# Random-feature attention and a two-layer network on one core: another order of the work, eight buffers for a tile's sums, and matmuls of 256 columns in the second layer

## The chip, the cores and the metric

The kernel runs on one core of a Trainium2 chip. A core has TensorE (matmuls, written PE in the profile, its weight loads PEld), VectorE (DVE), ScalarE (ACT), GpSimd (POOL), and SyncE (SP), whose queue issues every DMA of this kernel. The metric is the time of one execution on the device in microseconds (us). Three runs of the kernel before took 992.41, 993.01 and 994.23 us; the median, 993.01 us, is the number to compare with. A change of under 0.2% can hardly be told from none.

## The reference

For each of 8 batches and 8 heads, with 576 rows of 64 values, the reference computes attention through 128 random features, then a normalization and a two-layer network over all 4608 rows of 512 values, and adds the network's input to its output:

```python
def phi(x):
    proj = np.einsum('bhsd,md->bhsm', x, omega)
    h = proj - np.sum(x * x, axis=-1, keepdims=True) / 2.0
    h = h - np.max(h, axis=-1, keepdims=True)
    return np.exp(h) / np.sqrt(m)
q_p, k_p = phi(q * scale), phi(k * scale)
kv = np.einsum('bhsm,bhsd->bhmd', k_p, v);  z = np.sum(k_p, axis=2)
num = np.einsum('bhsm,bhmd->bhsd', q_p, kv)
x = num / (np.einsum('bhsm,bhm->bhs', q_p, z)[..., None] + 1e-06)     # then (8, 576, 512)
xn = (x - mean) / np.sqrt(var + 1e-06) * g_ln
out = x + np.maximum(xn @ w_ch1, 0.0) @ w_ch2                        # 512 -> 2048 -> 512
```

All of it is in float32 with random inputs.

## The kernel before

**Tiles.** The 4608 rows are cut into nine tiles of 512 rows (`t`), each of four chunks of 128 rows (`i`). The hidden layer has 2048 columns, sixteen blocks of 128 (`f`). The two layers are done in fp32r matmuls, each operand split into a rounded part and the remainder, and a product is three passes: rounded by rounded, and the two mixed ones.

**First layer.** Tiles 0 and 1 use it plainly (`mm1`, 12 matmuls of 512 columns per `f`). Tiles 2 to 8 use a seven-product scheme on 2 by 2 blocks (`seven`, `product` at L1033): seven operands made from the transposed rows (`ORDER`: B11, T2, T1, T3, B21, B22, N4) meet seven weight operands, three taken from the weights as they are and four from sums of weights. Each product is 6 matmuls of 256 columns. A block `(g, h)` gives two hidden blocks and takes 42 matmuls; a tile has eight such blocks.

**Second layer.** `mm2` (L1166) multiplies one hidden block with one block of the second weights: for each of four chunks three passes, 12 matmuls of 512 columns, all through the helper `rounded` (L989, recorded as L991). It adds up in four PSUM banks over all sixteen `f`; `result` (L1189) then adds `x`, frees the bank and stores.

**The weight sums.** `gen_sides` (L420) makes the four sums of first-layer weights for each of four groups `g` and two halves `k`, starting when the rows it reads are loaded. Its DVE work is at L432 (16 times), L439 (32) and, in `lesser`, L456 (16). The sums go to DRAM; `gen_ring` (L477) loads them again, sixteen loads of 512 KB per tile.

**Lent weights.** Some blocks of the second weights give up their place in SBUF after tile 1. `SHARED` lists them: the places of blocks 4, 5 and 6 hold operands of the seven products, that of 7 holds partial sums `u`, those of 2 and 3 hold staging buffers `y0` to `y3`. Each such block `a` then takes turns with block `a + 8` in the place of `a + 8`: both are stored once (`gen_leave`, L400) and loaded once per tile (`gen_return`, L406), issued from SP.

**From rows to operands.** The DVE normalizes a chunk (`gen_xnT`, L862). For tiles 2 to 8 `gen_turned` (L908) transposes it on PE (L917), ACT copies it into a `y` buffer (L922). Chunks come in the order 0, 2, 1, 3. With a pair (0, 2) or (1, 3) both there, four subtractions (L938) fill two more `y` buffers, and `parted` (L958) writes each of the seven operands as rounded part and remainder (L962 through the helper at L231 or L233, and L964) as soon as the operand's buffer is free from the tile before. Since one pair fills all four `y` buffers, chunks 1 and 3 wait until every operand has taken its part of the first pair.

**Attention of the next tiles** runs beside the network: `gen_q2` loads queries (L678), splits them (L683 on ACT, L685 on DVE) and multiplies with omega; `features` takes the maximum over partitions on GpSimd (`partition_all_reduce`, L714), subtracts it on DVE (L717) and takes the exponential on ACT (L720). `gen_k` does the keys (L617, L548, L554, L586), `gen_x` the quotient (L784 to L817).

**The order.** The program's instruction order on each engine is fixed before it runs, by a list scheduler (`Plan`). Every step is a generator that yields what it needs: a wait for a key, buffers, or time on an engine with a cost in us. `Plan.run` takes the earliest possible start on each engine and, among those ready, the lowest `rank`; where two engines can do a step, `starts` (L154) chooses. The costs shape only this order. On the chip each engine takes its instructions strictly in it, waiting on semaphores for what really is not ready. Ranks: the network's rectifications and sums -2000, the transposes -1000 and up, attention of tile `t` about 32t - 28, the weight sums 24 to 27, the network's matmuls 10000, so that these fill what is left of PE.

Of the kernel before, what the change touches and what calls it, by code (L numbers as in the profile page):

```python
# [68 lines left out]
class Plan:  # L69
# [10 lines left out]
    HOP = 0.2  # L80
    SAME = {ACT: 0.16, DVE: 0.13, POOL: 0.1}
    SLACK = 0.4
    FILL, IDLE = 10000, 20000
    HOLDER = 100
    BIAS = {PE: 0.0, ACT: 0.2, DVE: 0.5, POOL: -0.2, SP: 0.0}
# [67 lines left out]

    def starts(self, part, queue):  # L154

        times = ((max(part.ready(e), self.free_at[e]), e, cost) for e, cost in part.want[1].items())
        return min(times, key=lambda t: t[0] + t[2] + queue[t[1]])

    def run(self):
# [31 lines left out]
def favor_ffn(ctx, tc, kT, kTr, vF, vR, qT, qD, omT, gT, w1, w2, out):  # L191
# [27 lines left out]

    def dve(n, k=1, c=0.065):  # L220
        return "run", {DVE: k * (c + 0.00105 * n)}

    def us(eng, t):
        return "run", {eng: t}
# [195 lines left out]
    def gen_sides(g, k):  # L420


        for row in (k, k + 2):
            yield wait("w", 1, NK * g + row)
        if g + k:
            yield wait("read", *((g, 0) if k else (g - 1, 1)))
        tags = yield "get", n_big, 4
        low, high, a, b = (tile_of(x, [P, 2, HC], F32R) for x in tags)
        for x, row in ((low, k), (high, k + 2)):
            yield dve(DM)  # L430
            w = wparts[1, NK * g + row]
            nc.vector.tensor_tensor(out=f32(x), in0=f32(w[:, :, 0]), in1=f32(w[:, :, 1]), op=ALU.add)  # L432
        low, high, a, b = f32(low), f32(high), f32(a), f32(b)
        for out, left, right, op in (
            (a[:, 0], low[:, 1], high[:, 1], ALU.add), (a[:, 1], low[:, 0], low[:, 1], ALU.subtract),
            (b[:, 0], a[:, 0], low[:, 0], ALU.subtract), (b[:, 1], high[:, 0], b[:, 0], ALU.subtract),
        ):
            yield dve(HC)
            nc.vector.tensor_tensor(out=out, in0=left, in1=right, op=op)  # L439
        if (g, 0) not in sides:  # L440
            sides[g, 0] = dp.tile([P, 4, 2, 2, HC], F32, tag=f"side{g}", name=f"side{g}", bufs=1)
        done(("read", g, k))
        for n in range(2):
            plan.add(plan.cur.rank, halved(g, k, n, tags[n], tags[2 + n], (a, b)[n]))

    def halved(g, k, n, t_h, t_s, s):
        hi = tile_of(t_h, [P, 2, HC], F32R)
        eng = yield "run", {ACT: 0.56, DVE: 0.34}
        copy(eng, hi, s)
        yield dma(P * DM)  # L450
        nc.sync.dma_start(sides[g, 0][:, 2 * n : 2 * n + 2, 0, k], f32(hi))
        plan.add(plan.cur.rank, lesser(g, k, n, t_s, s, hi, t_h))

    def lesser(g, k, n, t_s, s, hi, t_h):
        yield dve(DM)
        nc.vector.tensor_tensor(out=s.bitcast(F32R), in0=s, in1=f32(hi), op=ALU.subtract)  # L456
        free(t_h)
        yield dma(P * DM)
        nc.sync.dma_start(sides[g, 0][:, 2 * n : 2 * n + 2, 1, k], s)
        free(t_s)  # L460
        done(("side", g, n, k))
# [210 lines left out]
    def gen_q2(blk, j, s):  # L672
        rank = plan.cur.rank
        q_turn = yield "get", turn["q"]
        t_q = yield "get", n_big
        qraw = tile_of(t_q, [P, 2 * QB])
        yield dma(P * 2 * QB)
        nc.sync.dma_start(qraw, qD[blk, j, s])  # L678
        yield wait("om2")
        t_s = yield "get", n_big  # L680
        qs = tile_of(t_s, [P, 2 * QB], F32R)
        yield act(2 * QB)
        nc.scalar.copy(out=qs, in_=qraw)  # L683
        yield us(DVE, 0.85)
        nc.vector.tensor_tensor(out=qs[D:P], in0=qraw[D:P], in1=f32(qs[D:P]), op=ALU.subtract)  # L685
        free(t_q, q_turn)
        t_b = yield "get", at_now()

        plan.cur.after = max(plan.cur.after, plan.cur.end + LATE)
        yield us(PE, 0.46)  # L690
        pq = bank(t_b)
        rounded(pq, om_hi, qs, start=True, stop=False)
        rounded(pq, om_lo, qs, start=False, stop=True)
        free(t_s)
        yield from features(blk, j, s, t_b, pq)
# [8 lines left out]
    def features(blk, j, s, t_b, pq):  # L704
        t_c = yield "get", n_big
        qc = tile_of(t_c, [P, 2 * QB])
        eng = yield "run", {ACT: 0.48, DVE: 0.62} if blk >= T // QB else {ACT: 0.58}
        copy(eng, qc, pq)
        free(t_b)
        mx_turn = yield "get", turn["mx"]  # L710
        t_m = yield "get", n_big
        mx = tile_of(t_m, [P, 2 * QB])
        yield us(POOL, 1.9)
        nc.gpsimd.partition_all_reduce(mx, qc, P, bass_isa.ReduceOp.max)  # L714
        done(("mx", blk, j, s))
        yield us(DVE, 0.95 if blk >= T // QB else 0.6)
        nc.vector.tensor_tensor(out=qc, in0=qc, in1=mx, op=ALU.subtract)  # L717
        free(t_m, mx_turn)
        yield act(2 * QB)
        nc.scalar.activation(out=qc, in_=qc, func=AF.Exp)  # L720
        phis[blk, j, s] = t_c, qc.rearrange("p (a b) -> p a b", b=QB)
        done(("phi", blk, j, s))
# [127 lines left out]
    def gen_xnT():  # L850
        for n in range(NC):
            t, i = divmod(n, TC)
            i = i if t < SEVEN else i // 2 + i % 2 * 2
            c = t * TC + i
            plan.cur.rank = URGENT + t
            yield wait("x", c)
            xn_turn = yield "get", turn["xn"]
            t_n = yield "get", n_big
            _, x, mu, rs = xs[c]
            xn = tile_of(t_n, [P, DM])  # L860
            yield us(DVE, 0.34)
            nc.vector.tensor_scalar(out=xn, in0=x, scalar1=mu, scalar2=rs, op0=ALU.subtract, op1=ALU.mult)  # L862
            done(("xn", c))
            if t >= SEVEN:
                plan.add(plan.cur.rank, gen_turned(t, i, xn, t_n, xn_turn))
                continue
            if i == 0:
                t_t = yield "get", n_xnT
                xnTs[t] = t_t, tile_of(t_t, [P, 2, NK, T], F32R)
            plan.add(plan.cur.rank, gen_xnT1(t, i, xn, t_n, xn_turn))  # L870
# [22 lines left out]
            op_at[f"o{i}"] = whole[:, i]  # L893
            free(f"o{i}")

    n_y, y_at = ("y0", "y1", "y2", "y3"), {}

    def gen_staged():
        yield wait("mm1", SEVEN - 1, 0)
# [7 lines left out]

    def gen_turned(t, i, xn, t_n, xn_turn):  # L908

        if i % 2:  # L910
            for name in ORDER:
                yield wait("x2", t, name, 0)
        t_b = yield "get", at_now()
        yield us(PE, 0.46)
        pt = bank(t_b).rearrange("p (a b) -> p a b", b=P)
        for k in range(NK):
# [7 lines left out]
        turned[t, i] = t_f, xf  # L924
        done(("turned", t, i))
        if i < 2:
            plan.add(plan.cur.rank, parted(t, "B11", i, xf[:, 0]))
            plan.add(plan.cur.rank, parted(t, "B21", i, xf[:, 1]))
            return
        i -= 2  # L930
        yield wait("turned", t, i)
# [5 lines left out]
        def less(out, left, right):  # L937
            nc.vector.tensor_tensor(out=out, in0=left, in1=right, op=ALU.subtract)  # L938

        rank = plan.cur.rank  # L940
        yield dve(HC)
        less(a[:, 0], xf[:, 0], xe[:, 0])
        yield dve(HC)
        less(a[:, 1], xf[:, 1], a[:, 0])
        plan.add(rank, parted(t, "T2", i, a[:, 1]))
        plan.add(rank, parted(t, "T1", i, a[:, 0]))
        yield dve(HC)
        less(c[:, 0], xf[:, 1], xf[:, 0])
        plan.add(rank, parted(t, "T3", i, c[:, 0]))
        plan.add(rank, parted(t, "B22", i, xf[:, 1]))  # L950
        yield dve(HC)
        less(c[:, 1], xe[:, 1], a[:, 1])
        plan.add(rank, parted(t, "N4", i, c[:, 1]))
        for name in ORDER:
# [3 lines left out]
    def parted(t, name, i, x):  # L958
        yield wait("op", t, name)
        o = ops[t, name][1]  # L960
        eng = yield "run", {ACT: 0.3, DVE: 0.28}
        copy(eng, o[:, 0, :, i * P : (i + 1) * P], x)  # L962
        yield dve(HC)
        nc.vector.tensor_tensor(  # L964
            out=o[:, 1, :, i * P : (i + 1) * P], in0=x, in1=f32(o[:, 0, :, i * P : (i + 1) * P]), op=ALU.subtract
        )
        done(("x2", t, name, i))

    def gen_xnT1(t, i, xn, t_n, xn_turn):
# [8 lines left out]
        pt = pt.rearrange("p k (a b) -> p k a b", b=BW)  # L978
        yield us(ACT, 0.5)
        nc.scalar.copy(out=xnT[:, 0], in_=pt)  # L980
        yield dve(DM)
        nc.vector.tensor_tensor(out=xnT[:, 1], in0=pt, in1=f32(xnT[:, 0]), op=ALU.subtract)  # L982
        free(t_b)
        done(("xnT", t, i))
# [141 lines left out]
    def halves(hl, cols, x):  # L1126
        yield act(x.shape[1], 1, 0.05)
        nc.scalar.activation(out=hl[:, 0, cols], in_=x, func=AF.Relu)  # L1128
        yield dve(x.shape[1])
        nc.vector.scalar_tensor_tensor(  # L1130
            out=hl[:, 1, cols], in0=x, scalar=0.0, in1=f32(hl[:, 0, cols]), op0=ALU.max, op1=ALU.subtract
        )
# [33 lines left out]
    def mm2(t, f):  # L1166
# [7 lines left out]
        for i in range(TC):  # L1174
            if f == 0:
                t_b = yield "get", (b_acc[i],)
                accs[i] = bank(t_b)
            yield us(PE, 3 * 0.225)
            cs = slice(i * P, (i + 1) * P)
            rounded(accs[i], hl[:, 0, cs], w[:, 0], start=(f == 0), stop=False)  # L1180
            rounded(accs[i], hl[:, 0, cs], w[:, 1], start=False, stop=False)
            rounded(accs[i], hl[:, 1, cs], w[:, 0], start=False, stop=(f == NF - 1))
            if f == NF - 1:
                plan.add(MOST_URGENT, result(t, i, accs[i]))
        free(t_h)
        if lent and t >= SEVEN - 1:
            free(*n_w[2, f + HOSTS if t >= SEVEN and f in SHARED else f])
# [85 lines left out]
WHOLE = 4  # L1273
LATE = 1.0
SEVEN, HC = 2, DM // 2
SHARED, HOSTS = (4, 5, 6, 7, 2, 3), 8
LENT = (*SHARED, *(f + HOSTS for f in SHARED))
LEAVE, RSIDE = 24, 24
WARM, COLD = 0.0, 5.0
# [47 lines left out]
```

## Time and profile before

| | |
|---|---|
| Median of three runs | 993.01 us |
| The profiled execution | 995.0 us |
| Its span, first to last instruction | 993.1 us |
| PE busy | 975.7 us (98%), 7816 matmuls |
| DVE busy | 680.4 us (69%) |
| ACT busy | 417.2 us (42%) |
| POOL busy | 139.7 us (14%) |
| DMA | 180.81 MB, 182 GB/s on average |
| Mean granted TensorE clock | 0.998 |

A row of a group reads: line, engine, operation, tiles written <- read, partitions x elements, count, then busy us, mean ns of one, and idle time before it. In a timeline row the first number is the start in us from the start of the span, the second the length to the end of the last instruction of the row. Matmuls overlap: one of 256 columns is shown as about 275 ns long although the next begins earlier, so the rate is read from starts, not from lengths. A row of the windows view gives, for one stretch, the busy us of the engines and in brackets the number of instructions, then the granted clock, the DMA share and GB/s.

### The profile page before, as it was taken

How to read it: one execution, taken by the hardware profiler on the slowest of the kernel's cores; microseconds unless marked ns; L12 is line 12 of the kernel's file. 1: busy time of each engine (PE TensorE's matmuls, PEld its weight loads, DVE VectorE, ACT ScalarE, POOL GpSimd, SP SyncE). 2: the span in 40 equal slices, each digit the busy share in tenths (PEclk: the TensorE clock that was granted, in tenths of full speed). 3: DMA queues.
4: the chain of work that ended last, by engine and by line, in shares of the span. 5: the costliest groups of instructions: out<-in, count | busy, mean ns of one | idle time of the engine just before them, and what ended most of it. 6: DMA issues, size and time to landing. Idle time of an engine off the chain costs nothing.

```text
span 993.1 us, 19831 instructions
## 1 busy us (share of the span) xinstructions
PE 975.7 (98%) x7816; PEld 839.3 (85%) x7816; DVE 680.4 (69%) x1530; ACT 417.2 (42%) x1009; POOL 139.7 (14%) x80
## 2 busy tenths in 40 slices
PE   9999998999999999999999999999999999999998
PEld 7888777877788888888888888988887989898897
DVE  6999999768667955797468845883578357345333
ACT  6588755534534544445234533342335132123111
POOL 5000422203301210023001400150014000000000
PEclk9999999999999999999999999999999999999999
DMA  9089635434365654755467545745574554557541
GB/s 357 8 292 387 221 123 178 140 121 115 126 199 164 223 181 142 239 175 177 142 226 252 182 149 162 233 134 196 175 248 146 173 191 150 170 163 260 169 151 43
DMA packets 68412, 180.81 MB, mean 182 GB/s; under 512 B 7264, under 2 KB 15584, under 8 KB 68320
## 3 DMA queue, kind: packets, MB, share of 16 engines
q1 hardware_dynamic: 68320, 179.55, 54.9%
q8 instruction: 62, 1.02, 0.4%
q14 instruction: 30, 0.25, 0.1%
HBM read 155.40 MB, written 24.12 MB: 181 GB/s over the span
## 4 chain that ended last, share of the span: by engine, by line
PE 85%; DVE 9%; DMA 3%; ACT 1%; issue 1%; SPq 0%; DVEq 0%
PE b L991 47%; PE b L1041 26%; PE b L784 3%; PE b L586 3%; PE b L617 3%; DMA wide<-qD 2%; DVE wide L685 1%; PE b L917 1%; DVE wide L717 1%; DMA w<-w 1%; DVE x L1193 1%; DVE wide L862 1%; DMA w<-kT 1%; PE b L657 0%; DVE xnT L982 0%
## 5 line engine op out<-in xcount | busy, mean ns | idle before, releaser
L991 PE MATMUL b<-w,hid 128*128 128x512 f32 x1728 | 434.3, 394 | 0.0
L991 PEld LDWEIGHTS b<-w,hid 128*128 128x128 f32 x1728 | 314.2, 188 | 62.2 <-issue 0.7
L714 POOL PARTITION_ALL_REDUCE wide<-wide x72 | 138.6, 1957 | 626.1 <-ACT wide L231 558.3
L1041 PE MATMUL b<-xnT,w 128*128 128x256 f32 x1344 | 178.6, 279 | 2.4 <-DVE w L1104 2.3
L1041 PEld LDWEIGHTS b<-xnT,w 128*128 128x128 f32 x1344 | 167.9, 188 | 8.8 <-DVE w L1104 3.3
L1104 DVE TENSOR_TENSOR w<-b,w 128x256 f32<-128x256 f32 x224 | 109.4, 489 | 49.7 <-PE b L1041 35.4
L1041 PE MATMUL b<-w,w 128*128 128x256 f32 x1008 | 129.0, 279 | 0.5 <-DVE w L964 0.5
L1041 PEld LDWEIGHTS b<-w,w 128*128 128x128 f32 x1008 | 124.4, 188 | 5.7 <-DVE w L964 0.7
L1130 DVE SCALAR_TENSOR_TENSOR hid<-w,hid 128x256 fp32r<-128x256 f32 x112 | 67.9, 606 | 74.7 <-ACT hid L1128 73.9
L1128 ACT ACTIVATE hid<-w 128x256 fp32r<-128x256 f32 x112 | 58.4, 528 | 135.3 <-PE b L991 69.0
L991 PE MATMUL b<-xnT,w 128*128 128x512 f32 x384 | 98.0, 395 | 1.3 <-ACT xnT L980 1.1
L554 ACT ACTIVATE kp<-b,mb 128x128 f32<-128x128 f32 x272 | 75.1, 388 | 48.6 <-DVE mb L548 48.6
L1130 DVE SCALAR_TENSOR_TENSOR hid<-b,hid 128x256 fp32r<-128x256 f32 x56 | 23.7, 424 | 91.0 <-ACT hid L1128 90.9
L991 PEld LDWEIGHTS b<-xnT,w 128*128 128x128 f32 x384 | 70.5, 188 | 18.2 <-ACT xnT L980 1.5
L1128 ACT ACTIVATE hid<-b 128x256 fp32r<-128x256 f32 x56 | 21.6, 386 | 147.0 <-PE b L991 134.9
L717 DVE TENSOR_TENSOR wide<-wide,wide 128x512 f32<-128x512 f32 x72 | 65.0, 904 | 5.5 <-POOL wide L714 5.1
L548 DVE TENSOR_REDUCE mb<-b 128x4 f32<-128x512 f32 x72 | 46.7, 683 | 24.1 <-PE b L617 24.0
L720 ACT ACTIVATE wide<-wide 128x512 f32<-128x512 f32 x72 | 45.5, 635 | 36.6 <-DVE wide L717 35.9
L685 DVE TENSOR_TENSOR wide<-wide,wide 64x512 fp32r<-64x512 f32 x56 | 43.3, 775 | 10.4 <-ACT wide L683 8.7
L784 PEld LDWEIGHTS b<-kv,wide 128*64 128x64 f32 (+1 forms) x1088 | 40.6, 140 | 8.5 <-issue 6.1
L231 ACT COPY wide<-b 128x512 f32<-128x512 f32 x67 | 38.5, 591 | 17.9 <-PE b L991 11.3
L784 PE MATMUL b<-kv,wide 128*64 128x65 f32 (+1 forms) x1088 | 45.3, 226 | 0.1
(89 smaller groups left out, 931.2 us busy)
## 6 DMA issues: line engine op xcount, KB each, us to landing
w<-side SPq DMA_DIRECT2D x112, 512.0 KB, 5.7
w<-kept SPq DMA_DIRECT2D x84, 512.0 KB, 3.5
w<-w SPq DMA_DIRECT2D x32, 512.0 KB, 7.1
wide<-qD SPq DMA_DIRECT2D x56, 256.0 KB, 3.6
out<-x SPq DMA_DIRECT2D x36, 256.0 KB, 3.1
side<-wide SPq DMA_DIRECT2D x32, 256.0 KB, 2.7
v<-vF SPq DMA_DIRECT2D x28, 260.0 KB, 4.2
wide<-kT SPq DMA_DIRECT2D x28, 256.0 KB, 4.2
```

The lines of the kernel that those rows point to most:

```text
L548: nc.vector.tensor_reduce(out=mb[:, 4 * s : 4 * s + 4], in_=pk, axis=AX.X, op=ALU.max, negate=True)
L554: nc.scalar.activation(out=kp[:, j], in_=pk[:, i], func=AF.Exp, scale=1.0, bias=mb[:, j : j + 1])
L685: nc.vector.tensor_tensor(out=qs[D:P], in0=qraw[D:P], in1=f32(qs[D:P]), op=ALU.subtract)
L714: nc.gpsimd.partition_all_reduce(mx, qc, P, bass_isa.ReduceOp.max)
L717: nc.vector.tensor_tensor(out=qc, in0=qc, in1=mx, op=ALU.subtract)
L720: nc.scalar.activation(out=qc, in_=qc, func=AF.Exp)
L784: nc.tensor.matmul(pn[a:z, i], phi(blk, h, slice(cols + a, cols + z)), kvs[b][1][:, h], start=True, stop=True)
L991: nc.tensor.matmul(out.rearrange("p (c a b) -> p c a b", a=AW, b=BW), lhsT, rhs.rearrange("p (a c b) -> p c a b", a=AW, b=BW), start=start ...
L1041: nc.tensor.matmul(passes(out), left(k, l), passes(right[:, r, k]), start=start and k + l + r == 0, stop=k + r == 2, skip_group_check=True,)
L1104: nc.vector.tensor_tensor(out=out, in0=left, in1=right, op=ALU.add)
L1128: nc.scalar.activation(out=hl[:, 0, cols], in_=x, func=AF.Relu)
L1130: nc.vector.scalar_tensor_tensor(out=hl[:, 1, cols], in0=x, scalar=0.0, in1=f32(hl[:, 0, cols]), op0=ALU.max, op1=ALU.subtract)
```

## The change

It has five parts. (1) `Plan.starts` lengthens a DVE step marked "port" while GpSimd is booked, up to a factor 2.2; `dve2` marks the steps that read two operands, and several fixed costs (0.85, 0.95 us) are replaced by it. (2) `gen_sides` waits for the last transposed chunk of tile 1 rather than for its weights. `halved` books the remainder before the store. (3) Blocks 0 and 1 join `SHARED`, so all sixteen second-layer blocks leave and return, and their places hold `y4` to `y7`; the wait of chunks 1 and 3 for the first pair's operands goes. (4) Ranks and lags: normalizing has rank 32t - 8 from tile 2 on, the transposes are booked 1 us later (`LATE`), `parted` has rank -1000 and `result` -950 except in the last tile. (5) From tile 2 on, `mm2` issues each matmul of 512 columns as two of 256, and books 0.2268 us for the pair.

```diff
+    SHARED = 2.2
...
     def starts(self, part, queue):
-        times = ((max(part.ready(e), self.free_at[e]), e, cost) for e, cost in part.want[1].items())
+        times = []
+        for e, cost in part.want[1].items():
+            t = max(part.ready(e), self.free_at[e])
+            if e == DVE and len(part.want) > 2:
+                both = min(max(self.free_at[POOL] - t, 0.0), cost * Plan.SHARED) if t > self.free_at[POOL] - 2.0 else 0.0
+                cost += both * (1 - 1 / Plan.SHARED)
+            times.append((t, e, cost))
...
+    def dve2(n, k=1, c=0.065):
+        return "run", {DVE: k * (c + 0.00105 * n)}, "port"
...
     def gen_sides(g, k):
-        for row in (k, k + 2):
-            yield wait("w", 1, NK * g + row)
+        yield wait("xnT", SEVEN - 1, TC - 1)
...
         copy(eng, hi, s)
+        plan.add(plan.cur.rank, lesser(g, k, n, t_s, s, hi))
         yield dma(P * DM)
         nc.sync.dma_start(sides[g, 0][:, 2 * n : 2 * n + 2, 0, k], f32(hi))
-        plan.add(plan.cur.rank, lesser(g, k, n, t_s, s, hi, t_h))
+        yield wait("lo", g, k, n)
+        free(t_h)
...
-        yield us(DVE, 0.85)
+        yield dve2(2 * QB)
         nc.vector.tensor_tensor(out=qs[D:P], in0=qraw[D:P], in1=f32(qs[D:P]), op=ALU.subtract)
...
-        yield us(DVE, 0.95 if blk >= T // QB else 0.6)
+        yield dve2(2 * QB) if blk >= T // QB else us(DVE, 0.6)
         nc.vector.tensor_tensor(out=qc, in0=qc, in1=mx, op=ALU.subtract)
...
-            plan.cur.rank = URGENT + t
+            plan.cur.rank = URGENT + t if t < SEVEN else NS * t - 8
...
-            yield us(DVE, 0.34)
+            yield ("run", {DVE: 0.45}, "port") if t >= SEVEN else us(DVE, 0.34)
...
-    n_y, y_at = ("y0", "y1", "y2", "y3"), {}
+    n_y, y_at = tuple(f"y{i}" for i in range(8)), {}
...
     def gen_turned(t, i, xn, t_n, xn_turn):
-        if i % 2:
-            for name in ORDER:
-                yield wait("x2", t, name, 0)
         t_b = yield "get", at_now()
+        plan.cur.after += LATE
         yield us(PE, 0.46)
...
-            plan.add(plan.cur.rank, parted(t, "B11", i, xf[:, 0]))
+            plan.add(URGENT, parted(t, "B11", i, xf[:, 0]))
...
-            yield us(PE, 3 * 0.225)
+            yield us(PE, 3 * 0.2268)
             cs = slice(i * P, (i + 1) * P)
-            rounded(accs[i], hl[:, 0, cs], w[:, 0], start=(f == 0), stop=False)
-            rounded(accs[i], hl[:, 0, cs], w[:, 1], start=False, stop=False)
-            rounded(accs[i], hl[:, 1, cs], w[:, 0], start=False, stop=(f == NF - 1))
+            if t < SEVEN:
+                rounded(accs[i], hl[:, 0, cs], w[:, 0], start=(f == 0), stop=False)
+                rounded(accs[i], hl[:, 0, cs], w[:, 1], start=False, stop=False)
+                rounded(accs[i], hl[:, 1, cs], w[:, 0], start=False, stop=(f == NF - 1))
+            else:
+                for l, r in ((0, 0), (0, 1), (1, 0)):
+                    for n in range(2):
+                        nc.tensor.matmul(
+                            accs[i].rearrange("p (c a b) -> p c a b", a=AW, b=BW)[:, :, n * 8 : n * 8 + 8], hl[:, l, cs],
+                            w[:, r, n * HC : (n + 1) * HC].rearrange("p (a c b) -> p c a b", b=BW, c=4),
+                            start=f + l + r + n == 0, stop=f == NF - 1 and l == 1, skip_group_check=True,
+                        )
             if f == NF - 1:
-                plan.add(MOST_URGENT, result(t, i, accs[i]))
+                plan.add(MOST_URGENT if t == NT - 1 else URGENT + 50, result(t, i, accs[i]))
...
-SHARED, HOSTS = (4, 5, 6, 7, 2, 3), 8
+SHARED, HOSTS = (4, 5, 6, 7, 2, 3, 0, 1), 8
```

The parts left out mark further DVE steps with `dve2` in place of `dve` (the sums of weights, the subtractions at L938, L964, L982 and L1130) and set the rank of the other `parted` steps to -1000.

More of the change, by code (lines that the diff above doesn't have):

```diff
@@ L429, in gen_sides @@
         for x, row in ((low, k), (high, k + 2)):
-            yield dve(DM)
+            yield dve2(DM)
             w = wparts[1, NK * g + row]
@@ L437, in gen_sides @@
         ):
-            yield dve(HC)
+            yield dve2(HC)
             nc.vector.tensor_tensor(out=out, in0=left, in1=right, op=op)
@@ L449, in halved, with lesser @@
         copy(eng, hi, s)
+        plan.add(plan.cur.rank, lesser(g, k, n, t_s, s, hi))
         yield dma(P * DM)
         nc.sync.dma_start(sides[g, 0][:, 2 * n : 2 * n + 2, 0, k], f32(hi))
-        plan.add(plan.cur.rank, lesser(g, k, n, t_s, s, hi, t_h))
-    def lesser(g, k, n, t_s, s, hi, t_h):
-        yield dve(DM)
+        yield wait("lo", g, k, n)
+        free(t_h)
+    def lesser(g, k, n, t_s, s, hi):
+        yield dve2(DM)
         nc.vector.tensor_tensor(out=s.bitcast(F32R), in0=s, in1=f32(hi), op=ALU.subtract)
-        free(t_h)
+        done(("lo", g, k, n))
         yield dma(P * DM)
@@ L926, in gen_turned @@
         if i < 2:
-            plan.add(plan.cur.rank, parted(t, "B11", i, xf[:, 0]))
-            plan.add(plan.cur.rank, parted(t, "B21", i, xf[:, 1]))
+            plan.add(URGENT, parted(t, "B11", i, xf[:, 0]))
+            plan.add(URGENT, parted(t, "B21", i, xf[:, 1]))
             return
@@ L938, in less @@
             nc.vector.tensor_tensor(out=out, in0=left, in1=right, op=ALU.subtract)
-        rank = plan.cur.rank
-        yield dve(HC)
+        rank = URGENT
+        yield dve2(HC)
         less(a[:, 0], xf[:, 0], xe[:, 0])
-        yield dve(HC)
+        yield dve2(HC)
         less(a[:, 1], xf[:, 1], a[:, 0])
@@ L946, in gen_turned @@
         plan.add(rank, parted(t, "T1", i, a[:, 0]))
-        yield dve(HC)
+        yield dve2(HC)
         less(c[:, 0], xf[:, 1], xf[:, 0])
@@ L950, in gen_turned @@
         plan.add(rank, parted(t, "B22", i, xf[:, 1]))
-        yield dve(HC)
+        yield dve2(HC)
         less(c[:, 1], xe[:, 1], a[:, 1])
@@ L962, in parted @@
         copy(eng, o[:, 0, :, i * P : (i + 1) * P], x)
-        yield dve(HC)
+        yield dve2(HC)
         nc.vector.tensor_tensor(
@@ L980, in gen_xnT1 @@
         nc.scalar.copy(out=xnT[:, 0], in_=pt)
-        yield dve(DM)
+        yield dve2(DM)
         nc.vector.tensor_tensor(out=xnT[:, 1], in0=pt, in1=f32(xnT[:, 0]), op=ALU.subtract)
@@ L1128, in halves @@
         nc.scalar.activation(out=hl[:, 0, cols], in_=x, func=AF.Relu)
-        yield dve(x.shape[1])
+        yield dve2(x.shape[1])
         nc.vector.scalar_tensor_tensor(
```

## The prediction

> **What bounds the kernel now.** I read the page's busy times first, then its chain of waits, then the windows view cut at the ends of the tiles.
>
> ```profile
> span 993.1 us, 19831 instructions
> PE 975.7 (98%) x7816; PEld 839.3 (85%) x7816; DVE 680.4 (69%) x1530; ACT 417.2 (42%) x1009; POOL 139.7 (14%) x80
> PE 85%; DVE 9%; DMA 3%; ACT 1%; issue 1%; SPq 0%; DVEq 0%
> ```
>
> ```profile
> 0.00:52.00 52.00, 50.55 (x473) 43.12 (x474) 43.01 (x107) 32.95 (x83) 16.71 (x16) 1.00 0.47 179
> 52.00:170.00 118.00, 115.50 (x811) 91.13 (x810) 114.94 (x226) 84.30 (x170) 21.33 (x11) 1.00 0.70 247
> 170.00:293.00 123.00, 121.54 (x998) 96.75 (x998) 87.25 (x192) 53.35 (x136) 25.38 (x13) 1.00 0.43 134
> 293.00:410.00 117.00, 116.05 (x1148) 99.93 (x1148) 84.90 (x198) 54.56 (x154) 14.62 (x8) 1.00 0.55 179
> 410.00:514.00 104.00, 103.28 (x879) 90.80 (x878) 71.46 (x165) 42.13 (x109) 15.18 (x8) 1.00 0.59 193
> 514.00:622.00 108.00, 106.76 (x964) 93.60 (x963) 73.95 (x173) 46.05 (x122) 15.00 (x8) 1.00 0.60 191
> 622.00:719.00 97.00, 95.00 (x690) 84.89 (x689) 62.27 (x146) 34.11 (x78) 15.73 (x8) 0.98 0.57 185
> 719.00:815.00 96.00, 93.03 (x686) 82.90 (x686) 61.50 (x144) 33.22 (x76) 15.79 (x8) 1.00 0.58 187
> 815.00:904.00 89.00, 89.00 (x646) 80.21 (x645) 47.20 (x124) 22.34 (x56) 0.00 (x0) 1.00 0.57 178
> 904.00:993.20 89.20, 85.03 (x536) 75.99 (x534) 33.93 (x67) 14.23 (x32) 0.00 (x0) 0.99 0.44 142
> ```
>
> The columns after the stretch's length are PE, PEld, DVE, ACT, POOL. PE is the bound from 52 us on: in the stretch 815 to 904 it has no gap at all. So the time can fall in two ways only: the matmuls come closer together, or PE's gaps close. The gaps are length minus PE busy: 2.5 and 1.5 us in the two stretches up to 293 us; then 0.95, 0.7, 1.2, 2.0 and 3.0 us for tiles 2 to 6. In the last stretch 4.2 us are missing, nearly all behind the last matmul, as its row shows: it ends at 989.4 of 993.1 us.
>
> ```profile
> 980.96 8.46 PE L991 MATMUL b<-w,hid 128*128 128x512 f32 x36
> ```
>
> The stretch at 622 us also has a granted clock of 0.98, which over 97 us costs about 1.9 us. DVE is the second bound, but only early: 115 of 118 us from 52 to 170.
>
> **The matmuls of 256 columns.** A busy PE says nothing of its rate, so I take starts from PE's timeline, first inside a tile without attention work, then in tile 1.
>
> ```profile
> 690.90 2.92 PE L991 MATMUL b<-w,hid 128*128 128x512 f32 x12
> 693.65 2.25 PE L1041 MATMUL b<-w,w 128*128 128x256 f32 x18
> 695.74 1.52 PE L1041 MATMUL b<-xnT,w 128*128 128x256 f32 x12
> 697.10 2.92 PE L991 MATMUL b<-w,hid 128*128 128x512 f32 x12
> 699.86 1.57 PE L1041 MATMUL b<-xnT,w 128*128 128x256 f32 x12
> 701.27 1.07 PE L991 MATMUL b<-w,hid 128*128 128x512 f32 x4
> ```
>
> ```profile
> 207.03 2.80 PE L991 MATMUL b<-w,hid 128*128 128x512 f32 x12
> 209.67 0.83 PE L991 MATMUL b<-xnT,w 128*128 128x512 f32 x3
> ```
>
> From 690.90 to 701.27 is one period, a block (g, h): 24 matmuls of 512 columns and 42 of 256 in 10.37 us. The 512s take 2.75 and 2.76 us per 12, 229 to 230 ns each. The 256s behind them take 2.09/18 = 116.1 ns, then, with no 512 just before, 1.36/12 = 113.3 ns, and once more behind 512s 1.41/12 = 117.5 ns. So a change of size costs the following group something, and a 512 here costs more than 2 x 113.3 = 226.7 ns. At 207 us the same form ran at 2.64/12 = 220 ns, so 229 is no property of 512 columns alone.
>
> After the change a period is 42 + 48 = 90 matmuls of 256. Their input form is that of the products; their output is written in runs of 64 rather than 8 elements, and two in a row go to different halves of a bank, in which I see nothing that costs. At 113.3 ns a period is 10.20 us, 0.17 us less. There are 7 tiles x 8 = 56 periods: **-9.7 us**. Bounds: all at 117.5 ns, the slowest group above, make 10.58 us, +0.21 us a period, +11.5 us. Downward, attention's small matmuls between the groups may cost less in re-starting than now; I allow -14. I take 113.3 because the group that follows no other size shows it.
>
> The Trainium skill speaks against this part. TensorE: Matmul & The Clock Gate, section Back-to-back issue gap, gives columns/2.4 plus 2.5 ns, so each split would add 2.5 ns, +3.4 us by estimate over 1344 splits. The trace disagrees with its size on both shapes (220 and 113.3 against 215.8 and 109.2), and here the unsplit ones do not reach their own best.
>
> **PE's gaps from tile 2 on.** They sum to 0.95 + 0.7 + 1.2 + 2.0 + 3.0 = 7.9 us, plus the 1.9 us of clock, which stands right behind the longest gap: 9.8 us. The largest gaps have PE standing at a transpose:
>
> ```profile
> 747.39 0.63 PE L917 MATMUL b<-ident,wide 128*128 128x128 f32 x4 [2.02 <-ACT wide L231]
> ```
>
> The releaser named is ACT, but in order of time it is the normalizing step (L862), which ends at 747.24 us, 0.15 us before the transposes. DVE is late because its steps are stretched while GpSimd takes its maxima:
>
> ```profile
> 636.50 0.69 DVE L685 TENSOR_TENSOR wide<-wide,wide 64x512 fp32r<-64x512 f32 x1
> 642.97 5.78 POOL L714 PARTITION_ALL_REDUCE wide<-wide  x3 [80.57 <-ACT wide L231]
> 644.80 1.51 DVE L685 TENSOR_TENSOR wide<-wide,wide 64x512 fp32r<-64x512 f32 x1
> ...
> 742.86 4.10 POOL L714 PARTITION_ALL_REDUCE wide<-wide  x2
> ...
> 745.24 1.53 DVE L1130 SCALAR_TENSOR_TENSOR hid<-w,hid 128x512 fp32r<-128x512 f32 x1
> 746.69 0.55 DVE L862 TENSOR_SCALAR wide<-x,st 128x512 f32<-128x512 f32 x1
> ```
>
> The same L685 takes 0.69 us alone and 1.51 beside the maxima, a factor 2.2, which is the constant of the new plan; L1130 just before the late step takes 1.53. The old plan books 0.85 us for it and 0.60 for L1130, so a stretch of such steps puts DVE one to two us behind, and PE, in its fixed order, meets a transpose whose rows are not there. The new plan books the stretch and puts the transposes 1 us (LATE) later still; meanwhile PE has the next network matmuls, which need neither. With eight buffers the transposes of chunks 1 and 3 come out of the tile's boundary too. Two things work the other way: normalizing loses its rank of about -1000 and queues behind its own tile's attention, and a new order has gaps of its own. Bounds: 0 and -9.8. I take half, **-5 us**.
>
> **Before tile 2.** The weight sums have these rows in the windows view of L432 and L439, and these in the timeline of tile 0's start:
>
> ```profile
> 0.00:52.00 52.00, 2.02 (x3) 1.00 0.47 179
> ...
> 0.00:52.00 52.00, 1.65 (x4) 1.00 0.47 179
> ```
>
> ```profile
> 43.91 0.66 DVE L432 TENSOR_TENSOR wide<-w 128x512 f32<-128x512 f32 x1
> ...
> 48.48 0.68 DVE L432 TENSOR_TENSOR wide<-w 128x512 f32<-128x512 f32 x1
> 49.09 0.54 DVE L862 TENSOR_SCALAR wide<-x,st 128x512 f32<-128x512 f32 x1
> ...
> 51.90 0.70 PE L991 MATMUL b<-xnT,w 128*128 128x512 f32 x2
> ```
>
> So 2.02 + 1.65 = 3.7 us of sums sit on DVE among the last normalizing steps before the first layer starts at 51.9 us; the one at 48.48 directly delays the last. They go, and weight conversions may fill part of the hole: bounds 0 and -3.7, I take -1.5. The 2.5 us of gaps up to 170 us come with DVE at 97%, and the sums leave that stretch too; the 1.5 us after it may grow, since the sums land there (DVE has 123 - 87 = 36 us free). Bounds +3 and -4, I take -1. Together **-2.5 us**.
>
> **Parts at nothing.** Four more blocks leave once, and 4 x 7 = 28 more loads return, on top of these:
>
> ```profile
> q1 hardware_dynamic: 68320, 179.55, 54.9%
> w<-kept SPq DMA_DIRECT2D x84, 512.0 KB, 3.5
> ```
>
> That is 32 x 0.52 = 17 MB, 5% more of the DMA engines, which are at 55 to 60% from tile 2 on. A block's place is free once block f + 8 of the tile before is done, eight `mm2` or four periods (41 us) ahead of its use; landing takes 3.5 us. SP issues in order, so a load that waits for its place also holds the loads of queries and weight sums behind it; the 41 us cover that. Without them, one landing a tile, 7 x 3.5 = 24 us. The results' lower rank holds four banks longer, which `mm2` of the next tile asks for only after a whole block of products (42 x 113.3 ns = 4.8 us). The last tile's results keep their rank, so the tail of 3.7 us stays.
>
> **The sum.** -9.7 - 5 - 2.5 = -17.2 us. The profiled execution took 995.0 us, its span and 1.9 us around it; so 977.8 profiled, and for the unprofiled runs, whose median is 993.0, 975.8: I say **976 us**.
>
> **Rivals.** *B: the order gives nothing.* New gaps take the place of the old; nothing but the rate changes: 993.0 - 9.7 = 983.3. For it: half of each gap term is my choice; against: the gaps' cause is in the rows and its size is booked now. *C: a fixed cost per matmul decides the split.* If the 512s are slow for a reason that 256s share, the split gains nothing and adds what a rate with a fixed part adds, between 0 and (226.7 - 220) = 6.7 ns x 1344 = 9 us; at a middle 3.5 us, 993.0 + 3.5 - 7.5 = 989. For it the 220 at 207 us; against it the 113.3 in the same tile as the 230. The rule of the skill above is of this kind. *D, slower: second-layer matmuls of 256 never settle* and hold the 117.5 ns that groups behind 512s show, through `hid` as weights or the halves in turn. Then 993.0 + 11.5 - 7.5 = 997. It decides from 10.37/90 = 115.2 ns on, where the split turns to a loss, and outweighs the closed gaps from 116.7. *E, slower too: the returns come late*, one landing a tile: 976 + 24 = 1000. Against it: the 41 us.
>
> **Chances.** The forecast has 0.58 (own range 967 to 983), B 0.20, C 0.10, D 0.07, E 0.05. The range for 8 in 10 takes in the forecast's bounds, B and C, and leaves out D and E: 966 to 992. A difference under 0.2%, 2 us, cannot be told from none; part of C may end there. Faster: 0.58 + 0.20 + 0.07 = 0.85; same 0.03; slower 0.12.
>
> **What would show it.** Right: a period in tile 6 or 7 near 10.2 us and 256-column matmuls 113 ns apart in `mm2`; PE gaps of 3 to 5 us in all from tile 2 on, none of 2 us at L917, clock 1.00 in every stretch; no L432 before 160 us and the first L991 near 50 us; returns landing well before their `mm2`. Wrong: `mm2` at 116 ns or more apart (C, D); PE waiting for the DMA of a returned block (E); gaps as large as before at other lines (B), above all between 170 and 293 us, where the sums now are.

## The result and the profile after

The changed kernel took 979.25 us (median of four runs, 977.56 to 979.78) against 993.28 us for the kernel before; the ratio is 0.9856, 95% interval 0.9839 to 0.9873. The forecast was 976 us in a range of 966 to 992. The sum was near; its largest term, as the experiments show, was wrong.

From the page of the profile after:

```profile
span 976.9 us, 22504 instructions
PE 967.8 (99%) x9146; PEld 895.0 (92%) x9146; DVE 681.5 (70%) x1536; ACT 412.0 (42%) x1003; POOL 140.5 (14%) x80
PE b L1196 27%; PE b L1050 24%; PE b L1000 20%; PE b L597 3%; PE b L628 3%; PE b L795 3%; DVE wide L728 2%; DVE wide L696 2%; DMA wide<-qD 1%; DVE w L947 1%; DVE w L1113 1%; DMA w<-side 1%; DVE hid L1139 1%; DVE wide L873 1%; PE b L926 1%
```

Lines have moved: L1196 is the second layer's split matmul, L1050 the products (L1041 before), L1000 the matmuls of 512 columns (L991), L926 the transposes (L917), L628 the keys (L617). The windows view of after, in the order length, PE, PEld, DVE, ACT, POOL:

```profile
0.00:52.00 52.00, 50.48 (x462) 42.66 (x463) 41.86 (x102) 32.56 (x82) 16.74 (x16) 1.00 0.58 215
52.00:170.00 118.00, 118.00 (x840) 94.14 (x839) 115.11 (x220) 81.35 (x164) 31.65 (x16) 1.00 0.61 219
170.00:293.00 123.00, 123.00 (x1030) 99.86 (x1029) 98.45 (x230) 54.83 (x141) 15.43 (x8) 1.00 0.57 185
293.00:410.00 117.00, 116.63 (x1354) 110.57 (x1354) 80.31 (x194) 52.72 (x149) 15.05 (x8) 1.00 0.64 209
410.00:990.00 580.00, 559.72 (x5468) 547.79 (x5466) 345.73 (x794) 190.53 (x468) 61.67 (x32) 1.00 0.60 196
```

The 4.0 us of PE's gaps between 52 and 293 us are gone. From 293 us on, 0.4 us are left and, of the 566.9 us that the last stretch really has, 7.2 us, of which the tail behind the last matmul is 3.7: together 3.9 us. Counted the same way the kernel before has 8.2; the 7.9 of the prediction leaves out its last stretch. The clock is 1.00 in every stretch. The first layer begins at 50.8 us instead of 51.9, the first product of tile 2 at 285.0 us instead of 293.7. The span is 16.2 us shorter, the median of the runs 14.0.

PE's timeline of after inside tile 5, two `mm2` and 42 product matmuls from 686.00 to 696.26:

```profile
686.00 2.88 PE L1196 MATMUL b<-w,hid 128*128 128x256 f32 x24
688.73 1.52 PE L1050 MATMUL b<-xnT,w 128*128 128x256 f32 x12
690.09 2.88 PE L1196 MATMUL b<-w,hid 128*128 128x256 f32 x24
692.80 2.20 PE L1050 MATMUL b<-w,w 128*128 128x256 f32 x18
694.85 1.58 PE L1050 MATMUL b<-xnT,w 128*128 128x256 f32 x12
696.26 2.88 PE L1196 MATMUL b<-w,hid 128*128 128x256 f32 x24
```

Here the forecast rate holds: 2.73/24 and 2.71/24 are 113 to 114 ns, and the period is 10.26 us against 10.37. It misses 10.20 by one wait of 60 ns in the group at 694.85. So the change did to a quiet period what was forecast, and the time fell as forecast. It would have been easy to stop here.

### The profile page after: what moved, and what is told of

It reads as the page before. It is cut to its first block, busy times and chain, and to the rows that moved or that the text cites. A ratio compares the mean times of both kernels' runs of the same rounds, so it can differ in the third digit from the quotient of the medians.

```text
span 976.9 us, 22504 instructions
## 1 busy us (share of the span) xinstructions
PE 967.8 (99%) x9146; PEld 895.0 (92%) x9146; DVE 681.5 (70%) x1536; ACT 412.0 (42%) x1003; POOL 140.5 (14%) x80
## 4 chain that ended last, share of the span: by engine, by line
PE 83%; DVE 12%; DMA 2%; ACT 1%; issue 1%; POOL 0%; SPq 0%; DVEq 0%
PE b L1196 27%; PE b L1050 24%; PE b L1000 20%; PE b L597 3%; PE b L628 3%; PE b L795 3%; DVE wide L728 2%; DVE wide L696 2%; DMA wide<-qD 1%; DVE w L947 1%; DVE w L1113 1%; DMA w<-side 1%; DVE hid L1139 1%; DVE wide L873 1%; PE b L926 1%
## 5 line engine op out<-in xcount | busy, mean ns | idle before, releaser
L1196 PE MATMUL b<-w,hid 128*128 128x256 f32 x2688 | 332.0, 277 | 0.0
L1196 PEld LDWEIGHTS b<-w,hid 128*128 128x128 f32 x2688 | 317.5, 188 | 4.2
L1050 PE MATMUL b<-xnT,w 128*128 128x256 f32 x1344 | 177.2, 278 | 2.4 <-DVE w L1113 1.5
L1050 PEld LDWEIGHTS b<-xnT,w 128*128 128x128 f32 x1344 | 163.7, 188 | 5.6 <-DVE w L1113 2.5
L1050 PE MATMUL b<-w,w 128*128 128x256 f32 x1008 | 129.7, 278 | 0.0
L1050 PEld LDWEIGHTS b<-w,w 128*128 128x128 f32 x1008 | 121.0, 188 | 2.0
L1139 DVE SCALAR_TENSOR_TENSOR hid<-w,hid 128x256 fp32r<-128x256 f32 x112 | 63.6, 569 | 76.6 <-ACT hid L1137 76.4
L1000 PE MATMUL b<-w,hid 128*128 128x512 f32 x384 | 98.5, 394 | 0.0
L1000 PE MATMUL b<-xnT,w 128*128 128x512 f32 x384 | 98.0, 394 | 0.1
L1000 PEld LDWEIGHTS b<-xnT,w 128*128 128x128 f32 x384 | 70.2, 188 | 15.8 <-issue 1.0
L1000 PEld LDWEIGHTS b<-w,hid 128*128 128x128 f32 x384 | 70.5, 188 | 15.1 <-issue 0.3
L728 DVE TENSOR_TENSOR wide<-wide,wide 128x512 f32<-128x512 f32 x72 | 61.1, 854 | 1.9 <-POOL wide L725 1.9
```

The costliest lines, as they stand in the source:

```text
L1000: nc.tensor.matmul(out.rearrange("p (c a b) -> p c a b", a=AW, b=BW), lhsT, rhs.rearrange("p (a c b) -> p c a b", a=AW, b=BW), start=start ...
L1050: nc.tensor.matmul(passes(out), left(k, l), passes(right[:, r, k]), start=start and k + l + r == 0, stop=k + r == 2, skip_group_check=True,)
L1139: nc.vector.scalar_tensor_tensor(out=hl[:, 1, cols], in0=x, scalar=0.0, in1=f32(hl[:, 0, cols]), op0=ALU.max, op1=ALU.subtract)
L1196: nc.tensor.matmul(accs[i].rearrange("p (c a b) -> p c a b", a=AW, b=BW)[:, :, n * 8 : n * 8 + 8], hl[:, l, cs], w[:, r, n * HC : (n + 1) ...
```

## The experiments

Every kernel is timed against the kernel before on its own chip. The instruction order is laid out anew for each, so an edit can move work also where it changes no line. The last columns are PE's gaps (length minus PE busy, us) and the granted clock in two stretches of the windows view: around the start of tile 2, and behind it.

| kernel | ratio to before (95%) | 280 to 340 us: gaps, clock | 340 to 960 us: gaps |
|---|---|---|---|
| before | 1 | 0.95, 1.00 | 7.3 |
| after | 0.9856 (0.9839 to 0.9873) | 0.3, 1.00 | 3.5 |
| after, split undone | 0.9858 (0.9840 to 0.9877) | 0.1, 1.00 | 1.1 |
| after, DVE costs undone | 0.9845 (0.9826 to 0.9863) | 0.0, 1.00 | 3.75 |
| after, ranks and lag undone | 0.9861 (0.9840 to 0.9883) | 0.0, 1.00 | 1.75 |
| after, weight sums early | 0.9902 (0.9883 to 0.9921) | 0.2, 1.00 | 2.35 |
| after, four buffers | 0.9925 (0.9910 to 0.9940) | 3.8, 0.94 | 2.5 |
| after, 256 columns everywhere | 0.9874 (0.9853 to 0.9895) | 0.3, 1.00 | 2.6 |
| before, split alone | 1.0004 (0.9989 to 1.0019) | 0.5, 1.00 | 9.4 |
| before, lag alone | 0.9973 (0.9964 to 0.9982) | 2.1, 1.00 | 2.7 |
| before, late sums alone | 1.0091 (1.0075 to 1.0107) | 10.2, 0.83 | 5.1 |
| before, eight buffers alone | 1.0065 (1.0042 to 1.0087) | 0.7, 1.00 | 7.8 |
| before, late sums and eight buffers | 1.0069 (1.0046 to 1.0093) | 8.8, 0.89 | 7.1 |
| before, those two, split and lag | 0.9945 (0.9928 to 0.9962) | 3.9, 0.94 | 4.1 |

**The split, undone and alone.** Theory: the prediction's term of -9.7 us. Rival: the split is worth little, and the gaps were everything.

```diff
-                for l, r in ((0, 0), (0, 1), (1, 0)):
-                    for n in range(2):
-                        nc.tensor.matmul(accs[i]..., hl[:, l, cs], w[:, r, n * HC : (n + 1) * HC]..., ...)
+            rounded(accs[i], hl[:, 0, cs], w[:, 0], start=(f == 0), stop=False)
+            rounded(accs[i], hl[:, 0, cs], w[:, 1], start=False, stop=False)
+            rounded(accs[i], hl[:, 1, cs], w[:, 0], start=False, stop=(f == NF - 1))
```

The whole matmuls are booked at 0.225 us again; alone in the kernel before, the split pair is booked at 0.2268 us.

> The kernel after, with the second layer's matmuls whole again (512 columns, booked at 0.225 us); order, buffers and ranks stay new. The prediction's term for the split (-9.7 us, a quiet period's 0.17 us times 56) expects this kernel 9 to 10 us slower than the kernel after: 0.995 of the kernel before. Counting PE's time by kind in the two traces gives the second layer and the products together only 4.6 us less after the change, of which about 1.2 us were the slow clock at 651 us: by that it is 3 to 5 us slower than after, 0.989 to 0.991. If the split gives nothing: 0.986. In the trace the 512s should run at 226 to 239 ns among the products, and the products behind them at 116 to 120.

> The kernel before with only the split (matmuls of 256 columns in the second layer from tile 2 on, booked at 0.2268 us for the pair). By the prediction's rival B 983.3 us, 0.990 of the kernel before. By the count of PE's time by kind 988 to 990 us, 0.995 to 0.997, with PE's gaps at the transposes as before (7 to 8 us from tile 2 on). If the split gives nothing without the new order: 1.000.

Measured: 0.9858 without it, 1.0004 with it alone. The split is worth nothing that can be told, at either end. Two readings of the traces say why. First, the rate. PE's timeline of after and of the kernel with whole matmuls, at the same place, behind the small matmuls of a key block:

```profile
429.00 1.16 PE L628 MATMUL b<-om,wide 64*128 64x128 f32 x16
430.10 3.05 PE L1196 MATMUL b<-w,hid 128*128 128x256 f32 x24
432.98 1.52 PE L1050 MATMUL b<-xnT,w 128*128 128x256 f32 x12
```

```profile
428.94 1.16 PE L628 MATMUL b<-om,wide 64*128 64x128 f32 x16
430.04 3.03 PE L1000 MATMUL b<-w,hid 128*128 128x512 f32 x12
432.90 1.31 PE L1050 MATMUL b<-xnT,w 128*128 128x256 f32 x10
```

From start to start 2.88 us split and 2.86 us whole: no gain. By the single starts in the trace, the first whole matmul behind the small ones takes 333 ns and the eleven others 230 on average, as in a quiet stretch; the first split one takes 226 and the eight behind it 116 to 124, before they come down to 113. So the split pays more for the restart, and that eats what it gains behind it. I added up the distances between starts of the second layer's matmuls and the products, from the first product on and idle time left out. Attention's small matmuls cut the network's into some 110 stretches. In the five long ones (over 200 matmuls of 256 columns, a 512 counted as two; some 2700 of 5040 in all) a matmul of 256 costs 115.5 ns in the kernel with whole matmuls and 114.0 in after; in stretches of 12 to 30 it costs 121.5 and 121.6. In sum 594.2 against 590.6 us: the rate is worth 3.6 us, not 9.7. Second, the gaps. Where PE meets a chain that is not its own, a faster PE should only wait longer. PE's timeline of the kernel with the split alone, at the gap of 2.0 us of tile 5 before:

```profile
648.63 0.63 PE L917 MATMUL b<-ident,wide 128*128 128x128 f32 x4 [2.75 <-DVE wide L862]
```

Its gaps from 340 to 960 us are 9.4 us against 7.3, and in after 3.5 against 1.1 with whole matmuls. That takes back 2 of the 4 us, and the intervals (about 2 us each way) cover the rest. Whether the faster PE or the new order made the gaps longer was not taken apart.

**The DVE costs.** Theory: booking the stretch beside GpSimd closed PE's gaps. Rival: something else did.

```diff
-        return "run", {DVE: k * (c + 0.00105 * n)}, "port"
+        return "run", {DVE: k * (c + 0.00105 * n)}
...
-        yield dve2(2 * QB)
+        yield us(DVE, 0.85)
```

(likewise 0.95 and 0.34 us again)

> The kernel after with the plan's old DVE costs: no lengthening beside GpSimd's maxima, and 0.85, 0.95 and 0.34 us booked again for the query's remainder, the subtraction of the maximum and the normalizing. If the booked stretch is what closed PE's gaps (the prediction's cause), gaps of 1 to 2 us at the transposes come back in tiles 2 to 6, 3 to 6 us in all: 0.989 to 0.992 of the kernel before. If the 1 us lag of the transposes or the buffers closed them: 0.985 to 0.987, as the kernel after.

Measured 0.9845: undone alone, the costs lose nothing. The gaps are not back.

**Ranks and lag.**

```diff
-            plan.cur.rank = URGENT + t if t < SEVEN else NS * t - 8
+            plan.cur.rank = URGENT + t
...
-        plan.cur.after += LATE
...
-                plan.add(MOST_URGENT if t == NT - 1 else URGENT + 50, result(t, i, accs[i]))
+                plan.add(MOST_URGENT, result(t, i, accs[i]))
```

(The ranks of `parted` are the old ones again too.)

> The kernel after with the old ranks of normalizing, operands and results and without the 1 us lag of the transposes. If ranks and lag carry the 9 us that are left: 0.993 to 0.996, with PE gaps of 1 to 3 us at the transposes in tiles 2 to 6. If the prediction's cause (the booked stretch) or the buffers do: 0.985 to 0.988. Sharing between the parts would show as 2 to 4 us here, 0.988 to 0.990.

Measured 0.9861: nothing either. That costs, ranks and lag can go singly does not yet make them idle; a kernel without costs and ranks stands further on.

**The lag alone**, one line added to the kernel before:

```diff
         t_b = yield "get", at_now()
+        plan.cur.after += LATE
         yield us(PE, 0.46)
```

> The kernel before with only the 1 us lag of the transposes in the plan (tiles 2 to 8). If that lag alone takes PE off its gaps of 2 us at the transposes of tiles 5 and 6 (4 us, and 2 us of slow clock behind them): 0.993 to 0.996 of the kernel before, clock 1.000. If DVE's lateness is as large as the lag or the gaps move to another line: 0.998 to 1.001.

Measured 0.9973, 2.7 us. From 340 to 960 us the gaps fall from 7.3 to 2.7 us, so standing at the transposes was a cause of them, as the prediction read; but 1.1 us come back at the start of tile 2.

**The weight sums, undone and alone.**

```diff
-        yield wait("xnT", SEVEN - 1, TC - 1)
+        for row in (k, k + 2):
+            yield wait("w", 1, NK * g + row)
```

(Only the wait is changed, here and in the kernels that add late sums to the kernel before. The other half of this part, by which `halved` books the remainder before the store, stays new here and old there.)

> The kernel after with the weight sums started as before, when their weights are there. The prediction priced this wait at 2.5 us in all: 0.988 of the kernel before. The first product begins 8.7 us earlier after the change (285.0 against 293.7 us); if the sums alone are the cause, this kernel loses 5 to 8 us: 0.991 to 0.994, the first layer starts at about 52 us and PE has gaps around 165 us again. If the other parts did it: 0.986.

> The kernel before with only the later start of the weight sums. If the parts add up, the 4.5 us that undoing it cost come back as a gain: 0.995 to 0.996 of the kernel before, first layer from about 51 us, no PE gap around 165 us. If the later sums crowd the stretch from 170 to 293 us without the new costs and ranks: 0.999 to 1.002. The prediction's 2.5 us would be 0.9975.

Undone in after, they cost 4.6 thousandths: the first layer starts at 52.1 us again and PE has 2.6 us of gaps up to 170 us. Alone in the kernel before, the later sums cost 9 us, a sign opposite to the one they have in the change. The windows view of that kernel at the start of tile 2, three stretches of 5 us (PE, granted clock, DMA share), and what PE waited for between 280 and 340 us (total us, times, longest):

```profile
285.00:290.00 5.00, 3.35 (x51) 1.00 0.32 121
295.00:300.00 5.00, 4.15 (x58) 0.50 0.52 186
305.00:310.00 5.00, 2.20 (x33) 0.50 0.97 247
```

```profile
PE b L1040 <- DMA w<-side: 2.0, 1, 2.0
PE b L783 <- DVE wide L455: 1.8, 1, 1.8
PE b L783 <- ACT kp L553: 1.5, 1, 1.5
```

The sums (L455, and the load of the stored sums) now stand where tile 2 needs them. PE gets gaps of 0.7 to 2.0 us in a row, and then the clock is halved for some 20 us, which stretches what is left of its work. This is what the prediction had priced at +3 at most.

**The buffers, undone and alone, and together with the sums.**

```diff
-    n_y, y_at = tuple(f"y{i}" for i in range(8)), {}
+    n_y, y_at = ("y0", "y1", "y2", "y3"), {}
...
+        if i % 2:
+            for name in ORDER:
+                yield wait("x2", t, name, 0)
...
-SHARED, HOSTS = (4, 5, 6, 7, 2, 3, 0, 1), 8
+SHARED, HOSTS = (4, 5, 6, 7, 2, 3), 8
```

> The kernel after with four staging buffers, six lent pairs and the wait of chunks 1 and 3 for the first pair's operands, as before; the rest is new. Split and DVE costs have been undone alone and moved nothing that can be told (0.9858, 0.9845), the early weight sums cost 4.6 thousandths (0.9902), so some 9 us of the 14 are still without a cause. If the buffers carry them: 0.993 to 0.996 of the kernel before, PE gaps at the tile boundary. If the prediction was right to price them at nothing: 0.985 to 0.987.

> The kernel before with only the eight staging buffers. If buffers gain by themselves what they gain in the kernel after: 0.993. If they gain only by making room for the later sums (the pair works, neither part does): 0.997 to 1.001, with PE's gaps at the transposes of tiles 5 and 6 as before.

> The kernel before with two parts of the change: weight sums later, and eight staging buffers (all sixteen blocks lent, chunks 1 and 3 not waiting). Alone the later sums cost 9 thousandths (1.0091); taken out of the kernel after, the sums cost 4.6 and the buffers 7 thousandths. If these two carry the change and only work together: 0.986 to 0.989 of the kernel before. If the buffers' effect in the kernel after hangs on the new ranks or costs as well: 0.993 to 1.000. If parts simply add (sums +9, buffers -7): 1.002.

Undone in after, the buffers cost 6.9 thousandths, the most of any part. The windows view of that kernel shows where:

```profile
280.00:340.00 60.00, 56.20 (x524) 52.32 (x519) 52.98 (x126) 29.05 (x69) 14.29 (x8) 0.94 0.62 202
```

It is again the start of tile 2: 3.8 us of gaps and a clock of 0.94, while behind 340 us it has fewer gaps than after. With eight buffers and the new order the same stretch lost 0.3 us. Alone in the kernel before, however, the buffers cost 6.5 thousandths, and with the late sums 6.9, with 8.8 us of gaps at the start of tile 2. My guess that these two make the pair that carries the change is false. Where the buffers alone lose their 6 us shows in small pieces: the span is 4.9 us longer in the profile, with 2.2 us more of PE's gaps, spread over the whole kernel, and a clock of 0.76 from 166 to 173 us, where before had 1.00. What in the buffers does this is open.

**What is needed besides.** The kernel before with sums, buffers, split and lag, that is the change without DVE costs, without ranks and without the new booking of the sums' remainder:

```diff
-        for row in (k, k + 2):
-            yield wait("w", 1, NK * g + row)
+        yield wait("xnT", SEVEN - 1, TC - 1)
...
+        plan.cur.after += LATE
```

(with the eight buffers and the split as in the change)

> The kernel before with later weight sums, eight buffers, the split into 256 columns and the 1 us lag of the transposes: the change without its DVE costs and without its ranks. Undoing these two alone moved nothing that can be told (0.9845 and 0.9861), so this should be at 0.983 to 0.987. If costs and ranks stand in for each other, so that one of them is needed: 0.989 to 0.993.

Measured 0.9945: 5.5 us gained, not 14. What is left shows at the start of tile 2 once more, in the waits of PE between 280 and 340 us:

```profile
PE b L1038 <- DMA w<-side: 3.0, 1, 3.0
```

A load of stored sums is late there. In the kernel without the costs, but with the ranks, the same stretch has no gap:

```profile
280.00:340.00 60.00, 60.00 (x702) 56.95 (x701) 38.75 (x105) 26.05 (x73) 8.28 (x4) 1.00 0.64 214
```

It is tempting to read this as costs and ranks standing in for each other: with the costs and neither ranks nor lag 0.9861, with ranks and lag and no costs 0.9845, with the lag and neither of the two 0.9945. But the first two also have the new booking of the remainder, and the third has the old, so the booking is as good a reading. No run has it alone.

**Which load is late.** The sums read the first-layer weights in eight passes (two adding steps at L441 each, L431 in the kernels with the old booking). Only when the last pass has read them, and tile 1's first layer is done with them, does `gen_move` free their last place, and into it goes the fourth load of stored sums, which tile 2 needs. The loads after it come later still. For after, and for the kernel of 0.9945, the adding steps from 160 to 245 us (DVE busy us and count) and the fourth load:

```profile
160.00:245.00 85.00, 9.27 (x14) 1.00 0.48 157
279.28 0.33 SPq L499 DMA_DIRECT2D w<-side  x1
```

```profile
160.00:245.00 85.00, 6.65 (x10) 1.00 0.45 145
292.90 0.33 SPq L487 DMA_DIRECT2D w<-side  x1
```

| kernel | adding steps done by 245 us, of 16 | fourth load issued | first product | clock, 280 to 340 us |
|---|---|---|---|---|
| after | 14 | 279.3 | 285.0 | 1.00 |
| after, DVE costs undone | 14 | 272.7 | 278.5 | 1.00 |
| after, ranks and lag undone | 14 | 278.9 | 287.6 | 1.00 |
| after, four buffers | 14 | 291.5 | 285.3 | 0.94 |
| before, those two, split and lag | 10 | 292.9 | 287.1 | 0.94 |
| before, late sums and eight buffers | 10 | 297.4 | 286.9 | 0.89 |
| before, late sums alone | 10 | 304.5 | 281.8 | 0.83 |

In the four kernels with a clock under 1.00 the fourth load is issued after the first product; in the ten others of the list, those with early sums among them, it has landed before it. PE's wait for a load of sums is named in two of the four (3.0 us in the kernel of 0.9945, 2.0 us with the late sums alone). In the kernel with four buffers the load lands 4.6 us after its issue, at 296.0 us, and PE's gap of 2.02 us ends at 296.15, though the profile names a DVE step of attention for it. There the eighth pass also stands on DVE between tile 2's subtractions (L950):

```profile
287.30 0.42 DVE L950 TENSOR_TENSOR w<-w 128x256 f32<-128x256 f32 x1
287.63 0.42 DVE L448 TENSOR_TENSOR wide<-wide,wide 128x256 f32<-128x256 f32 x1
287.96 0.42 DVE L950 TENSOR_TENSOR w<-w,w 128x256 f32<-128x256 f32 x1
288.30 0.42 DVE L448 TENSOR_TENSOR wide<-wide 128x256 f32<-128x256 f32 x1
```

Every kernel with late sums and the new booking has 14 steps done by 245 us, whether costs, ranks or buffers are undone; each of the three with the old booking has 10. So the booking goes with the pace of the sums. With four buffers it is the last pass alone that comes late, for a reason that no run shows.

**256 columns everywhere.** The first layer of tiles 0 and 1, and their second, in matmuls of 256 too:

```diff
+            for l, r in ((0, 0), (1, 0), (0, 1)):
+                for n in range(2):
+                    nc.tensor.matmul(ph...[:, :, n * 8 : n * 8 + 8], w[:, l, cs], xnT[:, r, k, n * HC : (n + 1) * HC]..., ...)
```

> The kernel after with every matmul of both layers in 256 columns, tiles 0 and 1 too (768 more are split). By the prediction's reading (512s at 230, 256s at 113.3 ns) 768 x 3 ns and more: 2 to 5 us faster, 0.981 to 0.984 of the kernel before. By the count of stretches in the traces (between attention's small matmuls both forms take 121 to 122 ns for 256 columns, only long stretches without them gain) nothing: 0.985 to 0.988, since tiles 0 and 1 have attention work throughout.

Measured 0.9874, no gain, as the count of stretches said: tiles 0 and 1 have attention throughout. No version tried can be told from the kernel after by being faster.

## Why the prediction was right, and where it was wrong

- *The matmuls of 256 columns, -9.7 us: wrong by its size.* The step that failed is the multiplication of one period's 0.17 us by 56 periods. The period was taken from a quiet part of tile 5 (the prediction calls it a tile without attention work, but its row from 622 to 719 us has eight of GpSimd's maxima), and nearly half of the network's matmuls stand in short stretches between attention's, where both forms cost about 121.5 ns for 256 columns. No row from such a stretch behind the start of tile 2 was read; the trace of before had them. The 220 ns at 207 us, which the prediction quotes, are of tile 1 and do not hold there: behind the same kind of small matmuls whole ones took 230 ns at 430 us. The rate is worth 3.6 us of PE, and in the runs' times nothing that can be told.
- *Rival C and the rule of the skill.* The Trainium skill's page TensorE: Matmul & The Clock Gate, section Back-to-back issue gap, has a fixed cost per matmul in its formula for an isolated one and would make the split a loss; 3.4 us by estimate from its figure. The runs show no such loss: undone 0.9858 against 0.9856, alone 1.0004. Nor do they show the gain. The rival came nearest to the truth on this part, and had a chance of 0.10.
- *PE's gaps from tile 2 on, -5 us: right by its size.* 8.2 us became 3.9, and the slow clock went (1.9 us by the prediction, 1.7 by the trace): about -6. The place was right too, since the lag of the transposes alone takes the later gaps from 7.3 to 2.7 us. The cause given first, the booked stretch of DVE, is not needed: without it the gaps stay closed. They stay closed without ranks and lag as well, so which part closes them in the changed kernel is not singled out.
- *Before tile 2, -2.5 us: too small.* The first layer starts 1.1 us earlier, and 4.0 us of gaps are gone. Undone, the sums cost 4.6 thousandths, about 4.5 us.
- *Parts at nothing: wrong for the buffers.* I priced them by the returns' DMA and asked only what they cost there. The returns were indeed no matter: no PE wait for a returned block stands in any list of waits quoted. But without eight buffers the changed kernel loses 6.9 thousandths, at the start of tile 2: the last pass of the sums comes 20 us later than in after (286.7 against 266.9 us), and with it the fourth load. The booking of the remainder was not priced at all.
- *The sum.* Split 0 instead of -9.7, sums and buffers more than -2.5: the errors of the terms cancelled, so that the number came so near is luck. In the two profiles the 16.2 us are made up of 8.3 us of PE's gaps, 1.1 us of the earlier first layer, 4.0 us in the second layer and the products from tile 2 on (1.7 of them the half clock for 3.4 us), and some 2.5 us in PE's other matmuls. B, that the order gives nothing and the rate stays, would have been the opposite of what happened.

The parts do not add. Undone singly they cost 0, 0, 0, 4.5 and 7 us; tried singly on the kernel before they give 0 (split), -2.7 (lag), +9 (sums) and +6.5 (buffers). The change as a whole is -14. What is shown is where this is decided: in the four kernels whose start of tile 2 has 3.8 to 10.2 us of gaps and a clock of 0.83 to 0.94, the fourth load of sums comes after the first product, and in no other. What is argued is which part brings it there: the booking of the remainder goes with the pace of the sums, and the buffers with their last pass, but the booking alone was not tried.

## What to carry to other kernels

A rate read in a quiet stretch holds for quiet stretches: before it is multiplied by a count, count how many of the instructions stand in such a stretch, and read the rate in the others as well. In a kernel whose order is laid out by a list scheduler, price the parts of a change together at the places where several chains meet, since a part can change its sign with the others; and test a part both ways, alone and undone, down to its last line, since half a part left in can hide what the other half does. When work is put off, look at when its last piece is done against when its first user starts. Making the bound engine faster ahead of a wait for another engine may only lengthen the wait.

## What the runs showed of the hardware

A matmul's rate did not follow from its size alone. 512 columns took 220 ns behind a block of 64-row matmuls at 207 us in the kernel before, but 230 behind such a block at 430 us in the kernel with whole matmuls, and 229 to 230 behind matmuls of 256 columns; what decides is not known from these runs. 256 columns settled at 113.3 ns whatever `mm2` they belonged to, but behind a block of small ones the first took 226 ns and the next eight 116 to 124. No run here shows the reason.

The clock fell at gaps shorter than I expected. With gaps of 0.7 to 2.0 us in a row it was 0.50 from 295 to 310 us in the kernel with the late sums alone, and it did not come back while small matmuls and gaps went on. The Trainium skill, TensorE: Matmul & The Clock Gate, section Why this matters for your kernels, warns of gaps over about 3 us between bursts. Here no single gap was that long, so several short ones close together, with small matmuls between them, were enough; the measurement decides. Nor did the length of one gap decide: in the kernel before, a gap of 2.00 us ending at 649 us was followed by a clock of 0.57 from 650 to 654 us, and one of 2.02 us ending at 747 us by 1.00 from 748 to 752 us.
